# Score products of a gated attention: eight tiles of 64x32 in place of four of 64x64

## The chip, the cores and the metric

The kernel runs on one core of a Trainium2 chip. The metric is the device time of one execution in microseconds (us); the time of a kernel is the median of its runs. TensorE multiplies matrices (its weight loads are shown as an engine of their own, PEld), VectorE (DVE), ScalarE (ACT) and GpSimd (POOL) work elementwise, and SyncE (SP) issues most DMAs. Matrix products land in PSUM, in eight banks of 128 partitions x 512 float32 values.

## The reference

Gated linear attention (batch 4, 8 heads, 768 positions, 48 values a head) is followed by a two-layer block with a piecewise activation:

```python
f = 1.0 / (1.0 + np.exp(-f_logit))
for t in range(S):
    state = f[:, :, t, :, None] * state + np.einsum('bhd,bhe->bhde', k[:, :, t], v[:, :, t])
    y[:, :, t] = np.einsum('bhd,bhde->bhe', q[:, :, t], state)
x = y.transpose(0, 2, 1, 3).reshape(B * S, H * D)          # 3072 x 384
h = x @ w_in                                               # 3072 x 2048
g = np.where(h >= 1, h, np.where(h <= -1, 0.0, (h + 1) ** 2 / 4))
return g @ w_out                                           # 3072 x 384
```

All of it is wanted to float32 accuracy.

## The kernel before, in words

The 768 positions are cut into six steps of 128 (`C`), for all four batches, so that a step has 512 columns (`N`). For each step the attention yields 512 rows of x, and the two-layer block follows as 16 units, one for each 128 of the 2048 hidden values: 96 units in all. A unit's first half (`unit_1`, line 265) multiplies x by a slice of `w_in`; ScalarE and VectorE apply the activation; its second half (`unit_2`, line 289) adds its product with a slice of `w_out` to three PSUM banks. x, the weights and the activations are split into a high and a low part of a reduced float32, so that each half has nine matmuls of 512 columns.

The recurrence is not run position by position. Keys and queries of a step are scaled by running products of the gate. Within blocks of 64 positions (`T`) the outputs come from masked products of keys with queries, across blocks from the state. The heads stand in pairs on the partitions, head 0 at 0 to 47 and head 1 at 64 to 111, and pairs are taken two at a time. For each two pairs of steps 1 to 5, that is ten times, these steps run on TensorE:

- `scores_of_two` (line 657), which the change touches: products of 64 keys with 64 queries, float32, for 2 pairs x 4 batches x 2 heads x 2 blocks of keys. A matmul loads the keys (48 rows for the head's values x 64 columns) and streams 64 queries. Block 0 of the keys goes to PSUM partitions 0 to 63 and block 1 to 64 to 127; head 0 goes to a bank lent by the units (`ph`) and head 1 to one of three banks of the attention's own (`pa`). Head and block fix the place in the array, so that the four matmuls of a batch lie on four different tiles of 64 rows and 64 columns. VectorE then multiplies by the mask (line 663).
- `begin` (line 712): masked products times values, for the part that crosses over, and `states_by_parts` (line 791), the state's new part, at a later visit.
- `outputs` (line 739, then line 712 again): queries times states, and the rest of the masked products times values.

`transpose_tensor` (line 676) turns the keys of four early pairs; later ones are turned on VectorE. Lines 579, 609, 821, 836 and 770 belong to step 0.

The order is worked out ahead by a planner (`Plan`): it has a cost for each kind of work (the table `COST`, where `both` stands for `scores_of_two`) and puts the operations of every engine in an order, TensorE's in the order in which the program adds them. Each visit of the attention stands after a given unit (`TURNS`, `VISITS`). From the fourth two pairs on, line 739, line 712 and line 657 follow one another in TensorE's order with nothing between. A float32 matmul is one row in the program's order; the profile records it as two matmuls, each with its weight load.

Of the kernel before, what the change touches and what calls it, by code (L numbers as in the profile page):

```python
# [22 lines left out]
B, H, S, D = 4, 8, 768, 48  # L23
# [7 lines left out]
HEADS = ((0, 48), (64, 112))  # L31
# [8 lines left out]
T = C // 2  # L40
# [14 lines left out]
            rows=316, turned_rows=150, scan=1140, dve=602, small=200, sums=467, gate=600, act=575, bits=660, round=485, copy=520, turned=412, sig=538, decay=226,  # L55
# [27 lines left out]
class Plan:  # L83
# [7 lines left out]
    def add(self, engine, cost, emit, *deps, kb=0, near=0):  # L91
        flat = []

        def spread(d):
            if isinstance(d, list):
                for e in d:
                    spread(e)
            elif d is not None and d not in flat:
                flat.append(d)

        spread(list(deps))
        cost, kind = COST[cost] if isinstance(cost, str) else cost, cost
        if engine == "PE":
            if self.tensor is not None and self.tensor not in flat:
                flat.append(self.tensor)
            small = kind in SMALL_PRODUCTS
            cost += (COST["last"] if small else COST["first"]) if small != self.small else 0
            self.small = small
        o = Op(engine, cost, emit, flat, kb, near)
        for d in flat:  # L110
            d.users.append(o)
        if engine == "PE":
            self.tensor = o
        self.ops.append(o)
        return o
# [66 lines left out]
def gla_moe(ctx: ExitStack, tc: tile.TileContext, ff, kqd, f0, vv, vad, vbd, wd, fixedd, gates, values, headsd, out):  # L182
    nc = tc.nc
# [38 lines left out]
    half, up, down, top_of = (const.tile([128, 1], F32, name=a) for a in ("half", "up", "down", "top_of"))  # L222
# [4 lines left out]
    def wide(a):  # L227
        return a.rearrange("r b c -> r (b c)")

    def part(t, k):  # L230

        return t[:, k * N:(k + 1) * N].rearrange("r (b c) -> r b c", b=B)
# [8 lines left out]
    def key(n, p, b):  # L241
        return part(kq[p], 0)[:, B - 1 - b]

    def query(n, p, b):
        return part(kq[p], 1)[:, b]
# [63 lines left out]
    def vec(cost, fn, *deps):  # L309
        return add("DVE", cost, fn, *deps)  # L310
# [141 lines left out]
    def old(n, *names, of=att):  # L452

        return [] if n < 0 else [of[n].get(k) for k in names]
# [104 lines left out]
    def blocks(n):  # L559

        return [(pairs[n][1], m) for m in range(B)]
# [66 lines left out]
    def by_block(t):  # L628

        return wide(t).rearrange("u (o t) -> u o t", t=T)  # L630

    def masked(n):

        return [by_block(t) for t in am[n // 2 % 2 * 2:][:2]]

    TILES = ((0, 0), (1, 1), (1, 0), (0, 1))

    def borrowed(k):

        return [(6, ph[(k + 1) % 2].rearrange("p (b c) -> p b c", b=B), [gs[k - 1]["3"]]), bank(2)]  # L640

    def freed(k, held, *by):

        lent[k + 1] = by[0]
        banks[held[1][0]] = [by[1]]

    def scores_of_two(n, k):

        c, d = att[n], att[n + 1]
        held = borrowed(k)  # L650

        def emit():
            for e in range(2):
                for m, (q, b) in enumerate(blocks(n + e)):
                    for k, h in TILES:
                        (a, z), half = HEADS[h], slice(T * k, T * k + T)
                        nc.tensor.matmul(by_block(held[h][1])[half, e * B + m], key(n + e, q, b)[a:z, half],  # L657
                                         query(n + e, q, b)[a:z, T * (1 - k):][:, :T], start=True, stop=True)

        c["sc"] = d["sc"] = add("PE", "both", emit, c["kq"], d["kq"], [h[2] for h in held])  # L660
        c["am"] = d["am"] = []
        for h, (b, ps, _) in enumerate(held):
            o = vec("dve", lambda h=h, ps=ps: nc.vector.tensor_tensor(
                out=masked(n)[h], in0=by_block(ps), in1=mask_t.rearrange("u (o t) -> u o t", o=1).broadcast_to([C, 2 * B, T]), op=ALU.mult),
                c["sc"], ready["mask_t"], old(n - 4, "y"), att[2]["y"], att[2]["st"])
            c["am"].append(o)
        freed(k, held, *c["am"])
# [372 lines left out]
    with tc.If(bad > 0):  # L1040
# [7 lines left out]
        with tc.For_i(0, S, 1) as t:  # L1048
            e, z, y = tmp
            vb, fkq, z = e[:R, 0:768], e[:R, 768:816], z[:R, 0:768]  # L1050
# [22 lines left out]
        with tc.For_i(0, NI, 1) as i:  # L1073
# [9 lines left out]
            for j in range(NJ):  # L1083
                s, a, hi, lo = (t[j % 2] for t in (ph, act, ghi, glo))
# [89 lines left out]
```

## Time and profile before

| what | value |
|---|---|
| median of three runs (lowest, highest) | 472.98 us (472.7, 473.71) |
| the profiled execution: its own time | 474.75 us |
| its span, first to last instruction | 472.9 us |
| mean granted TensorE clock | 0.996 |
| TensorE busy, matmul records | 463.3 us, 4551 |
| VectorE busy | 369.0 us |
| ScalarE busy | 265.2 us |
| the ten calls of line 657, one call | 1.11 to 1.16 us |

The span is what the profile shows between the first and the last instruction; the execution's own time has a little more around it. "PE" is TensorE's matmuls and "PEld" its weight loads. In the grouped view a row reads: line, engine, operation, output<-inputs, shapes, count, then busy us and the mean ns of one, then the idle time of the engine just before, and what ended it. A shape such as `48*64 48x64` is the loaded operand (48 rows, 64 columns), and then what is streamed. In the timeline a row begins with the start and the duration in us. In the view by stretches a row holds the stretch, its length, the busy time of the engines with their counts, the granted clock, and the DMA's share and GB/s.

### The profile page before, as it was taken

The page shows a single profiled execution, that of the slowest core. Times are in us where ns is not written, and L with a number is a line of the kernel's source. Part 1 is how long each engine was busy: PE and PEld are TensorE (multiplying, and loading weights), DVE is VectorE, ACT ScalarE, POOL GpSimd, SP SyncE. Part 2 cuts the span into 40 slices and gives each one's busy share as a digit, 9 for nine tenths or more (in the row PEclk, how much of TensorE's full clock was granted, in tenths as well). Part 3 has the DMA queues.
Part 4 walks back from the last instruction along what each step waited for, and adds up shares of the span by engine and source line. Part 5 has one row for each costly group of instructions (what it writes and reads, how often), then busy time and mean ns, then how long its engine had stood idle before and what let it go on. Part 6 is the DMA issues. An engine that isn't in the chain of part 4 may idle for free.

```text
span 472.9 us, 10962 instructions
## 1 busy us (share of the span) xinstructions
PE 463.3 (98%) x4551; PEld 378.2 (80%) x4551; DVE 369.0 (78%) x704; ACT 265.2 (56%) x483; POOL 25.1 (5%) x67
## 2 busy tenths in 40 slices
PE   8999999999999999999999999999999999999993
PEld 4787888888888888888888888888888888888883
DVE  6989998999999988999889879566675645655553
ACT  3589989964463654645545464645464445544451
POOL 4100010010000001002000002000000000000000
PEclk9999999999999999999999999999999999999998
DMA  8788858372030332401234050333113342422322
GB/s 295 241 265 277 271 159 282 119 195 77 11 115 34 104 77 80 147 2 46 60 86 136 1 171 22 104 70 107 68 47 90 91 93 82 150 86 90 89 89 74
DMA packets 21336, 54.39 MB, mean 115 GB/s; under 512 B 3328, under 2 KB 5504, under 8 KB 21280
## 3 DMA queue, kind: packets, MB, share of 16 engines
q1 hardware_dynamic: 21184, 53.53, 36.6%
q8 instruction: 37, 0.61, 0.5%
q14 instruction: 19, 0.16, 0.1%
q10 hardware_dynamic: 96, 0.10, 0.1%
HBM read 44.76 MB, written 4.72 MB: 105 GB/s over the span
## 4 chain that ended last, share of the span: by engine, by line
PE 91%; DMA 3%; DVE 2%; ACT 1%; issue 1%; SPq 0%; DVEq 0%; ACTq 0%
PE po L289 41%; PE ph L265 40%; DMA raw<-in_w 2%; PE pa L712 2%; PE pa L739 2%; PE ph L657 2%; DMA f<-in_f 1%; PE pa L791 1%; PE ph L791 1%; DVE w L487 1%; PE pa L657 0%; ACT bits L395 0%; PE pa L836 0%; DVE am L622 0%; PE pa L821 0%
## 5 line engine op out<-in xcount | busy, mean ns | idle before, releaser
L265 PE MATMUL ph<-x,w_hi 128*128 128x512 f32 x570 | 145.3, 390 | 0.2 <-ACT w_hi L401 0.2
L268 ACT ACTIVATE act<-ph,half 128x512 f32<-128x512 f32 x96 | 66.0, 687 | 118.0 <-PE ph L265 115.2
L265 PEld LDWEIGHTS ph<-x,w_hi 128*128 128x128 f32 x570 | 106.8, 188 | 23.1 <-ACT w_hi L401 0.6
L276 DVE SCALAR_TENSOR_TENSOR act<-ph,act 128x512 f32<-128x512 f32 x96 | 66.1, 688 | 60.0 <-ACT act L271 58.6
L279 ACT CAST ghi<-act 128x512 fp32r<-128x512 f32 x96 | 59.6, 621 | 57.9 <-DVE act L276 57.8
L289 PE MATMUL po<-ghi,w_hi 128*128 128x512 f32 x287 | 85.6, 400 | 0.4 <-ACT ghi L279 0.4
L289 PE MATMUL po<-ghi,w_lo 128*128 128x512 f32 x287 | 82.8, 390 | 0.0
L289 PE MATMUL po<-glo,w_hi 128*128 128x512 f32 x287 | 82.5, 389 | 0.0
L265 PE MATMUL ph<-x,w_lo 128*128 128x512 f32 x285 | 80.0, 389 | 0.0
L282 DVE TENSOR_TENSOR glo<-act,ghi 128x512 fp32r<-128x512 f32 x96 | 66.1, 688 | 15.8 <-ACT ghi L279 13.6
L690 DVE STREAM_TRANSPOSE kn<-kq 32x128 f32<-32x128 f32 x224 | 67.8, 303 | 3.6
L289 PEld LDWEIGHTS po<-ghi,w_lo 128*128 128x128 f32 x287 | 53.9, 188 | 11.5
L289 PEld LDWEIGHTS po<-glo,w_hi 128*128 128x128 f32 x287 | 53.9, 188 | 11.5
L265 PEld LDWEIGHTS ph<-x,w_lo 128*128 128x128 f32 x285 | 53.5, 188 | 11.1
L271 ACT ACTIVATE act<-act 128x512 f32<-128x512 f32 x96 | 60.7, 632 | 2.8
L289 PEld LDWEIGHTS po<-ghi,w_hi 128*128 128x128 f32 x287 | 52.1, 188 | 11.6 <-ACT ghi L279 0.6
L414 DVE TENSOR_REDUCE ok<-raw 128x1 f32<-128x512 f32 x48 | 31.4, 679 | 1.8 <-DMA raw<-in_w 1.5
L487 DVE TENSOR_TENSOR_SCAN w<-f,least_w 128x512 f32<-128x512 f32 (+1 forms) x18 | 20.7, 1157 | 2.1 <-ACT f L483 2.1
L491 POOL COPY end<-w 128x4 f32<-128x4 f32 (+1 forms) x20 | 8.4, 419 | 259.3 <-DVE w L487 259.1
L494 DVE TENSOR_TENSOR_SCAN f<-f,rec 128x512 f32<-128x512 f32 (+1 forms) x18 | 20.7, 1156 | 0.1
L395 ACT ACTIVATE bits<-raw,top_of 128x512 uint32<-128x512 fp8e4 (+1 forms) x25 | 18.5, 743 | 3.9 <-DMA raw<-in_w 3.9
L555 ACT ACTIVATE sd<-sd,kq 112x48 f32<-112x48 f32 x80 | 19.4, 325 | 0.0
(120 smaller groups left out, 381.6 us busy)
## 6 DMA issues: line engine op xcount, KB each, us to landing
raw<-in_w SPq DMA_DIRECT2D x21, 511.6 KB, 4.5
kq<-in_kq SPq DMA_DIRECT2D x18, 512.0 KB, 5.4
raw<-in_w SPq DMA_DIRECT2D x18, 512.0 KB, 3.6
out_y<-raw SPq DMA_DIRECT2D x17, 256.0 KB, 2.2
f<-in_f SPq DMA_DIRECT2D x16, 256.5 KB, 3.3
v<-in_v SPq DMA_DIRECT2D x10, 384.0 KB, 5.3
raw<-in_w SPq DMA_DIRECT2D x12, 256.0 KB, 3.0
kq<-kq SPq DMA_DIRECT2D x30, 64.2 KB, 2.7
```

The source lines that it names most:

```text
L265: nc.tensor.matmul(ps[:, to], w_in(w_hi if high else w_lo, j, kt), xt[:, kt, t, c], start=(n == 0), stop=(n == 8))
L268: nc.scalar.activation(a, ps, AF.Relu, bias=half, scale=0.5)
L271: nc.scalar.activation(a, a, AF.Square)
L276: nc.vector.scalar_tensor_tensor(out=a, in0=ps, scalar=1.0, in1=a, op0=ALU.max, op1=ALU.min)
L279: nc.scalar.copy(hi, a)
L282: nc.vector.tensor_tensor(out=lo, in0=a, in1=hi.bitcast(F32), op=ALU.subtract)
L289: nc.tensor.matmul(po[e][:, c], w_out(part, j, e), g[:, of], start=(j == 0 and n == 0 and c.start == 0), stop=(j == NJ - 1 and n == 2))
L414: seen.append(vec("dve", lambda z=z, op=op: nc.vector.tensor_reduce(out=ok[:, 1 + NG + z + c:2 + NG + z + c], in_=words_of(raw[2])[1].bitc ...
L487: s1 = vec(COST["scan"] if count == 1 else 602, lambda bwd=bwd, u0=u0, u1=u1: nc.vector.tensor_tensor_scan(out=wide(w[:, u0:u1]), data0=bw ...
L494: s2 = vec(COST["scan"] if count == 1 else 602, lambda fwd=fwd, b0=b0, b1=b1: nc.vector.tensor_tensor_scan(out=fwd, data0=fwd, data1=wide( ...
L555: nc.scalar.activation(ds[:, at + b * D:at + (b + 1) * D], state[:, p * B + b], AF.Copy, scale=whole(kq[p])[:R, b:b + 1])
L690: nc.vector.transpose(kn[n % 2][u:u + 32, ::-1, r:r + 32], src[:, :, u:u + 32])
```

## The change

Each matmul of `scores_of_two` with 64 keys becomes two of 32. `u` counts the four blocks of 32 keys, and `c` makes the head alternate, so that the eight matmuls of a batch go to eight tiles of 64 rows and 32 columns, in the order (0, 0), (3, 1), (1, 1), (2, 0), (0, 1), (3, 0), (1, 0), (2, 1) of block and head. The queries are the same 64 as before, `1 - u // 2` in place of `1 - k`. What is computed, where it lands in PSUM, and the masking are the same. A call has 64 matmuls in place of 32.

```diff
-                    for k, h in TILES:
-                        (a, z), half = HEADS[h], slice(T * k, T * k + T)
-                        nc.tensor.matmul(by_block(held[h][1])[half, e * B + m], key(n + e, q, b)[a:z, half],
-                                         query(n + e, q, b)[a:z, T * (1 - k):][:, :T], start=True, stop=True)
+                    for u, h in [(u, (u + c) % 2) for c in range(2) for u in (0, 3, 1, 2)]:
+                        (a, z), rows = HEADS[h], slice(32 * u, 32 * u + 32)
+                        nc.tensor.matmul(by_block(held[h][1])[rows, e * B + m], key(n + e, q, b)[a:z, rows],
+                                         query(n + e, q, b)[a:z, T * (1 - u // 2):][:, :T], start=True, stop=True)
```

The planner's costs are as they were, so the order of all other work is too: the rows of VectorE, ScalarE, GpSimd and SyncE are the same in both programs, and TensorE has 2723 rows where it had 2563. At the fourth call, where line 657 follows line 712 (`ph` and `pa` are PSUM banks, `kq` holds keys and queries, `am` masked products, `v` values), TensorE's order was:

```order
L712 MATMUL pa_107<-am_76,v 48x64
L712 MATMUL pa_108<-am_77,v 48x64
L657 MATMUL ph_110<-kq_70 64x64
L657 MATMUL pa_109<-kq_70 64x64
L657 MATMUL ph_110<-kq_70 64x64
L657 MATMUL pa_109<-kq_70 64x64
L657 MATMUL ph_110<-kq_70 64x64
```

and is now:

```order
L712 MATMUL pa_107<-am_76,v 48x64
L712 MATMUL pa_108<-am_77,v 48x64
L657 MATMUL ph_110<-kq_70 32x64
L657 MATMUL pa_109<-kq_70 32x64 x2
L657 MATMUL ph_110<-kq_70 32x64
L657 MATMUL pa_109<-kq_70 32x64
L657 MATMUL ph_110<-kq_70 32x64 x2
L657 MATMUL pa_109<-kq_70 32x64
```

The sizes are partitions x columns of the output. What stood as four rows of 64x64 for a batch is eight matmuls of 32x64 (x2 is two in a row on the same bank), and no instruction of another line has moved between them. At the end of the same call stood, of the second pair (`kq_71`), with the unit that follows:

```order
L657 MATMUL ph_110<-kq_71 64x64
L657 MATMUL pa_109<-kq_71 64x64
L289 MATMUL po_112<-ghi_88,w_hi 128x512
L289 MATMUL po_113<-ghi_88,w_hi 128x512
L289 MATMUL po_114<-ghi_88,w_hi 128x512
```

and stands now:

```order
L657 MATMUL pa_109<-kq_71 32x64
L657 MATMUL ph_110<-kq_71 32x64 x2
L657 MATMUL pa_109<-kq_71 32x64
L289 MATMUL po_112<-ghi_88,w_hi 128x512
L289 MATMUL po_113<-ghi_88,w_hi 128x512
L289 MATMUL po_114<-ghi_88,w_hi 128x512
```

The same unit follows, behind 64 matmuls of the call in place of 32.

## The prediction

> **What bounds the kernel now.** I read the page's engine totals and its chain first, to learn which engine a change has to move.
>
> ```profile
> span 472.9 us, 10962 instructions
> PE 463.3 (98%) x4551; PEld 378.2 (80%) x4551; DVE 369.0 (78%) x704; ACT 265.2 (56%) x483; POOL 25.1 (5%) x67
> q8 instruction: 37, 0.61, 0.5%
> PE 91%; DMA 3%; DVE 2%; ACT 1%; issue 1%; SPq 0%; DVEq 0%; ACTq 0%
> ```
>
> TensorE is busy for 98% of the span and makes 91% of the chain, so whatever its stream gains or loses in the changed step is gained or lost at the end; nothing else covers it. Two other numbers matter below: each of the 4551 matmul records has one weight load, so TensorE executes 9102 instructions, and 37 instruction fetches brought 0.61 MB, one fetch of 16.5 KB for some 250 instructions.
>
> The changed step is line 657. The grouped view and the view by stretches give its size.
>
> ```profile
> L657 PE MATMUL ph<-kq 48*64 48x64 f32 x320 | 11.3, 219 | 0.0
> L657 PEld LDWEIGHTS ph<-kq 48*64 48x64 f32 x320 | 10.3, 135 | 0.6 <-issue 0.4
> L836 PEld LDWEIGHTS po<-kn,v 128*32 128x32 f32 x8 | 0.8, 109 | 0.0
> ...
> 0.00:60.00 60.00, 1.16 (x64) 1.02 (x64) 1.00 0.82 270
> 140.00:165.00 25.00, 1.11 (x64) 1.03 (x64) 1.00 0.28 88
> ```
>
> The step runs ten times. Each call of 32 matmuls shows 64 records (a float32 matmul is recorded as two passes, each with its load) and takes 1.11 to 1.16 us. All ten are 11.3 us, 2.4% of the span: that is all there is to win, and nothing bounds a loss. Inside a call the timeline shows what sets the pace:
>
> ```profile
> 54.53 0.22 PE L657 MATMUL ph<-kq 48*64 48x64 f32 x1
> 54.53 0.22 PE L657 MATMUL pa<-kq 48*64 48x64 f32 x1
> 54.54 0.22 PE L657 MATMUL ph<-kq 48*64 48x64 f32 x1
> 54.55 0.22 PE L657 MATMUL pa<-kq 48*64 48x64 f32 x1
> 54.58 0.22 PE L657 MATMUL ph<-kq 48*64 48x64 f32 x1
> ...
> 54.99 0.22 PE L657 MATMUL ph<-kq 48*64 48x64 f32 x1
> ```
>
> Four records start within 20 ns, one on each tile (about 7 ns apart), and then all four tiles wait: the next four begin at 54.58. From 54.53 to 54.99 there are 8 rounds, 58 ns each. Two neighbouring steps with other shapes tell what a round consists of:
>
> ```profile
> 60.23 0.03 PE pa L791
> ...
> 60.86 0.03 PE pa L791
> ...
> 136.36 1.04 PE pa L739 x64
> 137.40 0.45 PE pa L712 x32
> ```
>
> Line 791 (48 columns loaded, 48 streamed) needs 45 ns a round (14 rounds from 60.23 to 60.86), line 712 (48 loaded, 64 streamed) 56 ns (0.45 us for 8 rounds). So the streamed columns set a round, and loading 64 columns instead of 48 adds about 2 ns.
>
> **The change part by part.** *The rounds.* 64 matmuls make 128 records and 128 loads in a call, twice as many, on eight tiles. Each tile still runs 16 records of 64 streamed columns: 16 rounds remain. With 32 columns to load, the streaming alone sets the round, as at line 712: 56 instead of 58 ns, over 15 rounds -0.04 us a call. Eight starts at 7 ns fill 53 ns of a 56 ns round, so they just fit; the last round's starts end 27 ns later than with four, +0.03 us. Halving the work of a tile's load buys nothing more, since the load already lies beside the streaming. Over ten calls: -0.15 us. If a round stayed at four starts, a call would need 32 rounds and 0.93 us more; that is the upper bound (a rival below).
>
> [...]
>
> *The change of tile size.* Seven of the ten calls follow line 712 directly, whose 48 columns stand on 64-column tiles; there the array now goes from 64- to 32-column tiles. Before, the loader never idled there (line 657 shows 0.4 us of "issue", once). The nearest rows:
>
> ```profile
> 19.38 0.14 PEld L836 LDWEIGHTS po<-act,v 128*32 128x32 f32 x2 [0.17 <-issue]
> ...
> L739 PEld LDWEIGHTS pa<-kq,y 48*48 48x48 f32 x320 | 5.2, 119 | 3.5 <-issue 3.5
> ```
>
> At 19.38 us the array goes from 64 to 32 columns and the loader idles 0.17 us; at line 739, coming from the full array, 0.35 us each of ten times, of which a 512-column matmul covers most. Bounds 0 and 0.35; I take 0.12, near the first row less the 0.04 between matmuls anyway: 7 x 0.12 = +0.8 us. The other three calls, and the exits, change tile size already.
>
> *The instruction stream.* This is the part that decides. The change adds 640 matmul records and 640 loads, 1280 instructions. Most of the program needs one instruction in 113 ns (9 matmuls and 9 loads in 2.04 us), but the bursts of lines 739, 712 and 657, seven of them, use 320 in 2.4 us and will use 448 in the same time. Instructions come in fetches of some 250, and the trace has one place where they did not come in time, just after the last burst:
>
> ```profile
> 354.86 0.30 PEld L265 LDWEIGHTS ph<-x,w_hi 128*128 128x128 f32 x2 [0.45 <-issue]
> ...
> GB/s 149 149 1043 298 0 0 0 0 1 0 0 0 0 0 0 0 0 0 0 0 0 0 0 0 0 0 0 0 0 0 0 0 0 0 0 0 0 0 0 0
> q8 instruction: 1, 0.02, 5.5%
> ...
> GB/s 0 0 0 596 0 0 0 0 0 0 0 0 0 0 0 0 0 0 0 0 0 0 0 0 0 0 0 0 0 0 0 0 0 0 0 0 0 0 0 149
> q8 instruction: 1, 0.02, 5.4%
> ```
>
> These two DMA windows are 352.3 to 353.4 and 355.9 to 357 us, 40 slices each. The first fetch starts in the third slice, 352.37; TensorE, in the middle of a unit of six matmuls with no wait in it, idles 0.45 us until 354.86; the next fetch follows at 356.0. I read this as two blocks of instructions: a fetch starts when the sequencer enters the second, and the sequencer stops if it reaches its end too soon. Starved, one block takes 3.6 us from fetch to fetch (1 us moving, 1.5 until the first instruction, 1.15 until the next fetch).
>
> The sequencer runs ahead of the array, and that lead is the cover:
>
> ```profile
> L657 PEldq EVENT_SEMAPHORE x1: 51/51/51, 101.6 to 101.6; - x1
> 101.83 0.64 PEld L289 LDWEIGHTS po<-glo,w_hi 128*128 128x128 f32 x3
> 102.51 1.32 PEld L265 LDWEIGHTS ph<-x,w_hi 128*128 128x128 f32 x6
> 103.87 0.64 PEld L265 LDWEIGHTS ph<-x,w_lo 128*128 128x128 f32 x3
> 104.87 0.13 PEld L657 LDWEIGHTS ph<-kq 48*64 48x64 f32 x1 [0.35 <-issue]
> ```
>
> It handled line 657's wait at 101.6 us, over 12 matmuls and their loads before the step, so it leads by some 30 instructions: 3.4 us in the long matmuls, 0.1 us inside a burst. A block that ends inside a burst therefore stalls TensorE. Where blocks end follows from the counts (matmuls before each of the seven bursts, and before the idle place):
>
> ```profile
> 0.00:136.28 136.28, 133.95 (x1410) 1.00 0.60 192
> 0.00:160.91 160.91, 158.58 (x1756) 1.00 0.55 175
> 0.00:193.67 193.67, 191.34 (x2138) 1.00 0.51 160
> 0.00:230.50 230.50, 228.17 (x2538) 1.00 0.45 143
> 0.00:275.49 275.49, 273.16 (x2974) 1.00 0.43 134
> 0.00:300.08 300.08, 297.75 (x3320) 1.00 0.41 129
> 0.00:349.16 349.16, 346.83 (x3742) 1.00 0.39 123
> 0.00:354.84 354.84, 352.51 (x3915) 1.00 0.39 122
> ```
>
> A block ends at instruction 2 x 3915 = 7830, the others at multiples of 256 from there (I take 256 as the round number nearest to 250). Each call ahead adds 128. So the bursts now begin at 3204, 4024, 4916, 5844, 6844, 7664 and 8636, and blocks end 18 and 274 instructions into the first, 222 and 478 into the second, then 98 and 354, 194 and 450, 218 and 474, 166 and 422, 218 and 474. The sequencer's own waits are in the stream but not in the counts; they move these places up by at most 20. Less the lead of 30, three bursts (the 1st, 3rd, 6th) hold a whole block, and the 4th ends one at its very end. The others finish their second block after the burst, behind 3.4 us of long matmuls that cover the wait.
>
> The price is 3.6 us less the time in which the burst uses the block: 7 ns an instruction in lines 739 and 712, 3.5 in line 657, less 0.1 of lead. First: 1.5 us to use, stall 2.0. Third: 1.3, stall 2.2. Sixth: 1.1, stall 2.4. Fourth: 1.0, less 1.3 of cover, stall 1.3. Together 7.9 us. A fetch can also meet data traffic: the one of 352.37 was due at 349.6 (the block before 7830 ends 60 instructions of 7 ns behind the 7484 of 349.16, less the lead), 2.8 us instead of 1.15, so 0 to 1.65 us more each; I take 0.3 for each of four, +1.2.
>
> **The sum.** -0.15 + 0.8 + 7.9 + 1.2 = +9.7 us. The profiled execution took 474.75 us with 1.85 outside its span, and becomes 484.5; the median of the runs is 472.98, 1.8 below it, and becomes **482.7 us**. Own range: without the fourth stall, and each other 0.4 shorter, 478.5; with the full delay of every fetch, 488.
>
> **The rivals.** *Fetches keep up* (chance 0.12): more than two blocks are held, and the idle 0.45 us at 354.86 had another cause. Then -0.15 + 0.8: 473.6 us, no measurable change. For it: one starved place in the whole trace. Against it: that place waited for nothing else, and the next fetch came after it and not before. [...]
>
> *Shorter loads win* (0.06), on the other side: the tile change drains for nothing, since the loader starts while other tiles still stream, and fetches keep up. From there the 0.04 us a call decides, at most 0.45 with no late last round: 472.5 us. Against it: the loader's idle 0.17 us at 19.38.
>
> *Eight tiles run no faster than four* (0.10): the starts of a round do not all fit, or loads and streams of four column tiles in the same 64 rows hinder each other. 640 more records at 58/4 = 14.6 ns: +9.3 us. Blocks are then used more slowly in line 657, stalls fall to some 1.6 x 3 + 0.6: 472.98 + 9.3 + 0.8 + 5.4 + 1.2 = 490 us. Against it: 7 ns starts; for it, the trace never shows more than four.
>
> **Chances.** The forecast has 0.68, and 0.04 stays for slight losses between (474 to 478). A measurement of this kernel tells 0.2% (0.95 us) from no change: slower 0.83, same 0.14, faster 0.03. The range that leaves out 2 in 10 goes from 473.5, half of the first rival, to 490.
>
> **What would show it.** Right: line 657 with 640 records for each bank at 32 columns, starts 7 ns apart in groups of eight, rounds of 56 ns; 42 fetches; idle "issue" of some 2 us inside line 657 in the bursts near 138, 197 and 305 us, with one behind a burst near 236, and none in the three single calls before 110 us. Wrong: calls of 1.1 us everywhere without such idle time (blocks are deeper), calls of 2 us everywhere (tiles or starts), or idle time in other bursts (my places are off).

## The result, and the profile after

| | before | changed |
|---|---|---|
| median (lowest to highest), us | 473.42 (472.7 to 474.16), 6 runs | 485.69 (484.18 to 487.71), 6 runs |
| ratio, 95% interval | | 1.0257 (1.0241 to 1.0273) |
| the profiled execution, us | 474.75 | 485.13 |
| its span, us | 472.9 | 483.4 |
| mean granted TensorE clock | 0.996 | 0.991 |

The change makes the kernel 12.3 us slower; 482.7 was forecast, +9.7. The profiled pair differs by 10.4 us. One run below counts as slow, one of the four with half the queries (489.27 us), and its ratio leaves that run out. Of the page of the changed kernel, the totals, the fetches and the chain; and of its grouped view, the changed line (the columns as before):

```profile
span 483.4 us, 12242 instructions
PE 470.7 (97%) x5191; PEld 383.3 (79%) x5191; DVE 368.9 (76%) x704; ACT 265.1 (55%) x483; POOL 24.9 (5%) x67
q8 instruction: 42, 0.69, 0.6%
PE 94%; ACT 2%; DMA 1%; issue 1%; DVE 1%; ACTq 0%
...
L657 PE MATMUL pa<-kq 48*32 48x64 f32 x640 | 15.8, 226 | 3.3 <-issue 3.3
L657 PE MATMUL ph<-kq 48*32 48x64 f32 x640 | 15.8, 226 | 0.0
```

640 matmuls and 640 loads more, and 5 fetches more, as the edit says. TensorE still is the chain. What is new is 3.3 us of idle time inside line 657, ended by nothing that the profile shows.

**The idle places.** Behind 45 us, TensorE's loader waits 0.35 us at each of some twenty changes of tile size, in both kernels. Apart from these it has four waits of more than 0.2 us, at the rows that begin with these loads (idle time in the brackets):

```profile
199.58 0.10 PEld L657 LDWEIGHTS ph<-kq 48*32 48x32 f32 x1 [1.83 <-issue]
...
239.48 0.19 PEld L289 LDWEIGHTS po<-ghi,w_lo 128*128 128x128 f32 x1 [0.91 <-issue]
...
287.58 0.19 PEld L265 LDWEIGHTS ph<-x,w_lo 128*128 128x128 f32 x1 [0.27 <-issue]
...
310.79 0.12 PEld L657 LDWEIGHTS pa<-kq 48*32 48x32 f32 x1 [1.77 <-issue]
```

Two are inside the calls of the third and the sixth burst, one lies behind the fourth, as forecast; the first burst has none, and one behind the fifth was not forecast. How many matmuls had started by then is in the view by stretches:

```profile
0.00:199.00 199.00, 196.59 (x2639) 1.00 0.49 158
0.00:239.20 239.20, 236.00 (x3151) 1.00 0.43 141
0.00:287.30 287.30, 283.82 (x3661) 1.00 0.42 134
0.00:310.00 310.00, 305.64 (x4045) 1.00 0.39 126
```

In instructions (the loads counted one by one, 5279, 6302, 7323 and 8090, and 7830 at the idle place of the kernel before) these are 150 to 159 modulo 256. The trace also has the sequencer's own waits, 33, 34, 37 and 38 up to these places and 42 up to the old one. With them all five are 192 modulo 256 exactly. The fetches count the same: 5 more for 1280 instructions more is one for 256. So I take 256 for the size of a block, with TensorE run dry at the end of one each time.

**The calls.** The same view for line 657 alone; in the second and third stretch stand calls of the fifth and the third burst (1.11 us each before, 1.16 in the first stretch):

```profile
0.00:60.00 60.00, 1.48 (x128) 1.32 (x128) 1.00 0.80 273
280.00:290.00 10.00, 1.49 (x128) 1.32 (x128) 1.00 0.54 184
195.00:205.00 10.00, 1.75 (x128) 1.44 (x128) 1.00 0.40 147
```

A call is 0.32 us longer where it stands alone and 0.38 in a burst (fifth burst), although nothing is idle there; the third burst's 1.75 us hold one of the idle places, at which the call runs dry and fills again. Its timeline shows why (start, duration; x2 is two in a row):

```profile
360.67 0.24 PE L657 MATMUL ph<-kq 48*32 48x64 f32 x1
360.67 0.25 PE L657 MATMUL pa<-kq 48*32 48x64 f32 x2
360.69 0.24 PE L657 MATMUL ph<-kq 48*32 48x64 f32 x1
360.69 0.24 PE L657 MATMUL pa<-kq 48*32 48x64 f32 x1
360.70 0.25 PE L657 MATMUL ph<-kq 48*32 48x64 f32 x2
360.71 0.24 PE L657 MATMUL pa<-kq 48*32 48x64 f32 x1
360.75 0.22 PE L657 MATMUL ph<-kq 48*32 48x64 f32 x1
```

Eight start within 50 ns, the next eight begin at 360.75, and the two rounds from there take 57 and 55 ns: eight tiles do run together, in the 56 ns of a round at line 712. That lasts for some 32 matmuls and their loads. From then on the eight starts of a round take some 67 ns or more (from the trace, the rounds of this call: 79, 57, 55, 76, 148, 66, 67, 78, 102, 67, 66, 68, 94, 85, 67 ns).

**The way in.** Line 712 starts 0.45 us before line 657 in the kernel before (276.43 to 276.88) and 0.56 us now:

```profile
281.84 0.63 PE L712 MATMUL pa<-am,v 64*48 64x64 f32 x32
282.40 0.24 PE L657 MATMUL ph<-kq 48*32 48x64 f32 x1
```

**The clock.** In the view by stretches, the third column behind the length is the clock that TensorE was granted:

```profile
305.00:309.00 4.00, 4.00 (x219) 1.00 0.15 20
311.10:314.20 3.10, 3.10 (x18) 0.51 0.73 177
314.20:320.00 5.80, 5.80 (x27) 1.00 0.39 69
```

At the idle place of 310.8 the clock is halved for 3.4 us (310.72 to 314.13 in the trace); seven long matmuls fall into it, most of which start 0.427 us apart instead of 0.226.

**The sum of the profiled pair.** Three lone calls 3 x 0.32 = 1.0; seven in bursts 7 x (0.38 + 0.11) = 3.4; lesser delays in three of them, 0.4 (the first burst's call shows 1.76 us, two others 1.54 and 1.56); idle places 4.8 less the 0.45 of before, 4.3; half clock 7 x 0.2 = 1.4. Together some 10.5 us, and the span grew by 10.5. That they meet so closely is luck: the profiled run of the changed kernel reached its first call 0.7 us earlier (53.45 against 54.13 us), so that 0.6 us of what comes after has no term here.

### The profile page after: what moved, and what is told of

It is laid out like the page before. It is cut to its first block, busy times and chain, and to the rows that moved or that the text cites. A ratio compares the mean times of both kernels' runs of the same rounds, so it can differ in the third digit from the quotient of the medians.

```text
span 483.4 us, 12242 instructions
## 1 busy us (share of the span) xinstructions
PE 470.7 (97%) x5191; PEld 383.3 (79%) x5191; DVE 368.9 (76%) x704; ACT 265.1 (55%) x483; POOL 24.9 (5%) x67
## 4 chain that ended last, share of the span: by engine, by line
PE 94%; ACT 2%; DMA 1%; issue 1%; DVE 1%; ACTq 0%
PE po L289 41%; PE ph L265 39%; PE pa L712 2%; PE ph L342 2%; PE pa L739 2%; PE ph L657 2%; PE pa L657 1%; DMA raw<-in_w 1%; PE pa L791 1%; PE ph L791 1%; PE ph L609 1%; PE ph L864 0%; ACT bits L395 0%; PE po L579 0%; PE pa L836 0%
## 5 line engine op out<-in xcount | busy, mean ns | idle before, releaser
L289 PEld LDWEIGHTS po<-glo,w_hi 128*128 128x128 f32 x287 | 54.1, 189 | 11.5
L265 PEld LDWEIGHTS ph<-x,w_lo 128*128 128x128 f32 x285 | 53.5, 188 | 11.3 <-issue 0.3
```

The costliest lines, as they stand in the source:

```text
L265: nc.tensor.matmul(ps[:, to], w_in(w_hi if high else w_lo, j, kt), xt[:, kt, t, c], start=(n == 0), stop=(n == 8))
L289: nc.tensor.matmul(po[e][:, c], w_out(part, j, e), g[:, of], start=(j == 0 and n == 0 and c.start == 0), stop=(j == NJ - 1 and n == 2))
```

## The experiments

Two theories stood against each other. **F**: instructions come too slowly, at the end of a block (fetch) and within a call (dispatch). **T**: the tiles are slow, eight of 32 columns hinder each other. Where a median of the kernel before is needed, it is that of the same chip: 473.77 us for the first four runs, 473.71 for the next two.

### The same program, 64 instructions later

```diff
+    def first():
+        warm(12)
+        for _ in range(32):
+            nc.tensor.matmul(ph[1][:, 0:1], zeros, zeros[:, 0:1], start=True, stop=True)
-    add("PE", 4000, lambda: warm(12), set_zeros)
+    add("PE", 4000, first, set_zeros)
```

> The changed kernel with 32 one-column matmuls of zeros (64 instructions) more in the warm-up, before the first product, where TensorE waits for data. Theory F (instructions do not come in time: blocks of 256, and a stall where a block begins and ends inside a burst): every block now ends 64 instructions earlier in the program, so a whole block lies in the second, fourth, fifth, sixth and seventh burst and no longer in the third. Five stalls of 1.9 us (9.5 us) in place of the present 4.6 us: 490.6 us against 485.7, and the idle places still stand at an instruction count of 192 modulo 256, the sequencer's waits counted. Theory T (the loss is in the tiles: eight tiles of 32 columns hinder each other): nothing changes, 485.7 us, and the idle places stay in the same calls.

Measured: 496.13 us, ratio 1.0491 (1.0455 to 1.0526). The idle rows of its loader (the changed line is 662 here), and the matmuls started by then:

```profile
167.99 0.10 PEld L662 LDWEIGHTS ph<-kq 48*32 48x32 f32 x1 [1.26 <-issue]
...
202.10 0.10 PEld L662 LDWEIGHTS ph<-kq 48*32 48x32 f32 x1 [1.43 <-issue]
...
242.90 0.10 PEld L662 LDWEIGHTS pa<-kq 48*32 48x32 f32 x1 [1.33 <-issue]
...
290.04 0.10 PEld L662 LDWEIGHTS ph<-kq 48*32 48x32 f32 x1 [1.52 <-issue]
...
316.37 0.10 PEld L662 LDWEIGHTS pa<-kq 48*32 48x32 f32 x1 [1.50 <-issue]
...
368.77 0.10 PEld L662 LDWEIGHTS ph<-kq 48*32 48x32 f32 x1 [2.48 <-issue]
```

```profile
0.00:202.00 202.00, 196.64 (x2640) 1.00 0.48 155
0.00:242.80 242.80, 236.27 (x3151) 0.99 0.43 138
0.00:289.90 289.90, 282.03 (x3661) 0.99 0.41 129
0.00:316.30 316.30, 307.03 (x4045) 0.99 0.39 124
```

The places moved in the program and did not move in the count: 3151, 3661 and 4045 matmuls again, though what stands there is 64 instructions earlier in the program. All six are at 192 modulo 256 with the waits. The second, fourth, fifth, sixth and seventh burst stall as expected; the third, which I expected to be spared, stalls too (its block begins 43 instructions into the burst, just behind my lead of 30). Idle time is 9.5 us in place of 4.8. Of the 6.9 us by which the profiled execution (492.0) exceeds that of the changed kernel, 4.7 are these, where I expected 4.9. Another 2.1 lie ahead of the first call, which begins at 55.6 us instead of 53.5. The added matmuls are hardly the reason: they start between 5.8 and 6.5 us, and TensorE is only 0.3 us behind the changed kernel at 26 us. It then waits for ScalarE, which had itself waited 3.1 us for a weight transfer:

```profile
40.68 0.50 PE L289 MATMUL po<-ghi,w_hi 128*128 128x512 f32 x1 [1.89 <-ACT ghi L279]
```

That is not the effect that was asked for: without an edit there, the first call of the other runs began anywhere from 52.5 to 54.1 us. The median lies 10.4 us above that of the changed kernel and 5.5 above F. The profiled run was the fastest of the four: 492.0, 494.49, 497.76 and 499.36 us went with mean clocks of 0.993, 0.987, 0.983 and 0.980, so part of what the profiled run does not show is half clock; how much, no trace here tells. T has no answer to the idle places.

### Half the queries, three quarters of them

```diff
-                        nc.tensor.matmul(by_block(held[h][1])[rows, e * B + m], key(n + e, q, b)[a:z, rows],
-                                         query(n + e, q, b)[a:z, T * (1 - u // 2):][:, :T], start=True, stop=True)
+                        nc.tensor.matmul(by_block(held[h][1])[rows, e * B + m, 0:32], key(n + e, q, b)[a:z, rows],
+                                         query(n + e, q, b)[a:z, T * (1 - u // 2):][:, :32], start=True, stop=True)
```

> The changed kernel with 32 queries streamed in place of 64 in line 657; the other half of each product is left out. Theory F with a dispatch of some 5 ns an instruction: as many instructions, so a call still lasts 1.25 us from first to last start, and the stalls stay: 485.2 us. Theory T (streams of eight tiles hinder each other, a call is bound by what it streams): a call falls from 1.27 to some 0.9 us, 7 ns a start, and the kernel by 10 x 0.37 us to 482 us or less.

Measured: 485.75 us (481.59 to 489.27), ratio 1.0208 (1.0167 to 1.0248): halving what the tiles stream wins nothing that can be told from the times. The calls by themselves, and the starts in one of them:

```profile
280.00:290.00 10.00, 1.29 (x128) 1.18 (x128) 1.00 0.59 197
...
285.05 0.23 PE L657 MATMUL ph<-kq 48*32 48x32 f32 x3
285.08 0.21 PE L657 MATMUL pa<-kq 48*32 48x32 f32 x2
...
285.31 0.23 PE L657 MATMUL ph<-kq 48*32 48x32 f32 x3
```

From 285.05 to 285.31 stand 32 matmuls, 8.3 ns each; the trace has ten rounds of 66 or 67 ns in a row, 16 instructions of 4.17 ns. The same loads and matmuls need less while they are queued (the second and third round of this call take 40 and 32 ns), so I read this as the pace at which instructions are handed out. A call fell by 0.17 us to 1.10 from first to last start, where F said 1.25 and T 0.9: read so, dispatch is the floor, and what is streamed adds to it. The ten calls gave back 1.7 us, and the idle places took it: 1.70, 2.80, 2.10 and 0.51 us, 7.1 in place of 4.8. The longest:

```profile
241.65 0.19 PEld L289 LDWEIGHTS po<-ghi,w_lo 128*128 128x128 f32 x1 [2.80 <-issue]
```

What the streaming adds was asked again with 48 queries (the same edit with 48 in place of 32):

> The changed kernel with 48 queries streamed in place of 64 (the last 16 columns of each product are left out). If the 0.17 us by which a call with 64 queries is longer than one with 32 comes from streaming that nearly fills a round (56 of 67 ns), 48 queries (45 ns) leave room and a call takes 1.10 us. If it grows with what is streamed: 1.18 us.

1.17 us from first to last start (the first rounds 67, 47 and 42 ns, the last ten 67 with an 85, a 71 and an 81 between): the extra grows with what is streamed, 0.17 us at 64 columns, 0.08 at 48. Of the 0.17 us, 0.07 stand in the first three rounds (191 ns against 125; the second and third take 57 and 55 against 40 and 32); nothing in the fourth and fifth together (224 against 223); and 0.09 in the last ten, most of it in two neighbouring rounds of each four. Why there, no run tells. 484.8 us in one run.

### Twice the matmuls on four tiles

```diff
-                    for k, h in TILES:
+                    for k, h in TILES + TILES:
```

> The kernel before with every matmul of line 657 issued twice on its tile of 64x64: as many instructions as the change has, without eight tiles or 32 columns. Theory F: a call takes 32 rounds of 58 ns, +0.93 us, +9.3 us in all; the blocks end at the same instructions as in the changed kernel, so that TensorE stalls in the third and sixth burst for some 1.5 us each (the calls are longer and hide more), 473.4 + 9.3 + 3 = 486 us, with idle places at 192 modulo 256 again. Theory T: only the rounds are longer, 482.7 us, and no idle time inside a call.

Measured: 488.02 us, ratio 1.0297 (1.0279 to 1.0315), 2 us above F. Its idle places:

```profile
202.22 0.13 PEld L657 LDWEIGHTS pa<-kq 48*64 48x64 f32 x1 [1.66 <-issue]
...
242.34 0.19 PEld L289 LDWEIGHTS po<-ghi,w_lo 128*128 128x128 f32 x1 [0.52 <-issue]
...
291.02 0.19 PEld L265 LDWEIGHTS ph<-x,w_lo 128*128 128x128 f32 x1 [0.35 <-issue]
...
314.47 0.13 PEld L657 LDWEIGHTS ph<-kq 48*64 48x64 f32 x1 [1.62 <-issue]
```

These are the four places of the changed kernel, at the same instructions (5279, 6302, 7323, 8090), without eight tiles, without 32 columns and without a change of tile size. More instructions in the burst are enough. 4.2 us of idle time where I expected 3 makes somewhat over half of the difference.

### Half the matmuls on narrow tiles

```diff
-                    for u, h in [(u, (u + c) % 2) for c in range(2) for u in (0, 3, 1, 2)]:
+                    for u, h in [(u, u % 2) for u in (0, 3, 1, 2)]:
```

> The changed kernel with four of the eight matmuls of a batch (one head for each block of 32 keys; the other four are left out): as many instructions as before, on tiles of 32 columns. Theory F: only the change of tile size is left, seven times 0.16 us (the first start comes 0.11 us later, and the first round is not hidden, 0.05): 474.5 us, calls of 0.95 us from first to last start. Theory T: tiles of 32 columns are slow themselves, so that half of the loss stays: 479 us.

Measured: 474.38 us, ratio 1.0014 (1.0001 to 1.0027). Line 712 starts 0.55 us before line 657 (0.45 before), a call shows

```profile
340.00:360.00 20.00, 1.10 (x64) 0.94 (x64) 1.00 0.18 55
```

and no long idle place is left, the old one of 0.45 us included. So narrow tiles and the way into them cost some 0.6 us net (0.05 to 1.3 by the interval); nearly all of the loss is in the number of instructions. Only four of the eight tiles are used here; that eight run together is shown by the rounds of 56 ns, not by this run.

### The calls moved away from the bursts

```diff
-VISITS = {..., 10: (23, 25, 28), 12: (28, 32, 35), 14: (35, 41, 43), 16: (43, 47, 53), 18: (53, 56, 58), 20: (58, 64, 69), 22: (69, 73, 74)}
+VISITS = {..., 10: (24, 25, 28), 12: (29, 32, 35), 14: (36, 41, 43), 16: (44, 47, 53), 18: (54, 56, 58), 20: (59, 64, 69), 22: (70, 73, 74)}
```

> The changed kernel with line 657 of the last seven calls one unit later than lines 739 and 712, so that 18 long matmuls and their loads stand between them; as many instructions, the same eight tiles. Theory F: no block lies wholly in a burst any more (192 instructions, then 256 behind 3.4 us of long matmuls): the idle places of 1.9, 1.8, 0.6 and 0.2 us and the half clock behind one of them go, and the calls keep their 1.27 us, which is dispatch at 4.2 ns an instruction. Against the same move made to the kernel before (next run): +10 x 0.32 = +3.2 us, 478 us. Theory T (the tiles, or the calls by themselves, cause the idle time): it moves along with the calls, 486 us.

> The kernel before with the same move, as a control: seven more changes of tile size on the way in (0.10 us each, as a call behind line 265 shows) and out (0.11), less the 0.3 us of the one idle place: 473.5 + 1.5 - 0.3 = 474.7 us by either theory.

Measured: 480.85 us for the changed kernel, ratio 1.0151 (1.0131 to 1.0171), 476.99 for the kernel before, ratio 1.0063 (1.0046 to 1.008). Both are 2 to 3 us above what I expected. Some 1.1 us of it is an omission: the second way out of a burst also costs 0.11 us at the unit's first matmul (in the trace 0.337 us until the second one starts, 0.226 between others), and the first round of the call is no longer hidden, 0.05, seven times each. The rest I did not trace. The difference of the two is 3.9 us, of the profiled pair 3.4, where F said 3.2. In the grouped view of the changed kernel with its calls apart:

```profile
L657 PEld LDWEIGHTS ph<-kq 48*32 48x32 f32 x640 | 13.5, 105 | 3.1 <-issue 2.5 <-DVE kn L690 0.4
```

The 2.5 us are seven changes of tile size of 0.35 us; no long wait is left in the timeline, and the clock stays whole. The three calls that stood alone before take 1.48 us as in the changed kernel. Of the seven that were moved, one does, and six take 1.51 to 1.74; here the longest and that of 1.48:

```profile
165.00:171.00 6.00, 1.74 (x128) 1.51 (x128) 1.00 0.63 144
283.00:289.00 6.00, 1.48 (x128) 1.32 (x128) 1.00 0.77 269
```

Together the six have 0.7 us more, short delays inside the calls that F did not have; with the 3.2 they come to 3.9. With as many instructions on the same tiles, the change costs 3.9 us here and 12.3 in the bursts.

### Another order of the eight

```diff
-                    for u, h in [(u, (u + c) % 2) for c in range(2) for u in (0, 3, 1, 2)]:
+                    for u, h in [(u, c) for c in range(2) for u in range(4)]:
```

> The changed kernel with another order of the eight matmuls of a batch: the four blocks of keys of head 0, then those of head 1. What is asked is the length of a call that stands alone (1.27 us from first to last start in the changed kernel, 1.10 with half the queries, 0.94 before). If dispatch alone sets it: 1.27 us again. If matmuls that follow one another on the same 64 rows hinder each other: longer, 1.4 us or more.

1.27 us from first to last start again, round by round within 2 ns of the changed kernel. This order of the tiles changes nothing. The single run took 487.51 us; its trace has two stretches of half clock, behind each of the two long idle places:

```profile
200.40:203.80 3.40, 3.40 (x9) 0.51 0.76 244
313.40:316.50 3.10, 3.10 (x8) 0.50 0.64 159
```

## Why the prediction was right, and where it was off

*The bound.* Right: TensorE carried the chain before and after, and what its stream lost, the span lost.

*The instruction stream.* My reading, blocks of 256 and a stall where a whole block falls inside a burst, is borne out in the main: by long idle places at 192 modulo 256 in every run that has them, by their staying at the count when the program is shifted, by their coming back on four tiles, and by their going when the calls are moved away. That two blocks are held was an estimate from one idle place; it fits every place, and no run asked it by itself.

The size was off. I took 7.9 us for four stalls (2.0, 2.2, 2.4, 1.3) and 1.2 for data traffic; the profile has 1.8, 1.8, 0.9 and 0.3. The first stall did not come, and its fetch was early: the DMA view of the changed kernel has the packet in slice 21 of 40 between 135.5 and 136.35 us, before the burst began (136.6 us).

```profile
GB/s 0 0 0 0 0 0 0 0 0 0 0 0 0 0 0 0 0 0 0 0 771 0 0 0 0 0 0 0 0 0 0 0 0 0 0 0 0 0 0 0
q8 instruction: 1, 0.02, 7.2%
```

This block begins 37 instructions into the burst, at 136.85 us; if its fetch starts when the sequencer comes to the block, as I read it, the lead is more than my 30 instructions at times. The burst did not go free: its call shows 1.76 us instead of 1.49. The others were smaller since calls use up a block at 5 ns an instruction, not 3.5, which hides more.

*The rounds.* This is the step that failed: "Eight starts at 7 ns fill 53 ns of a 56 ns round, so they just fit", -0.15 us over ten calls. The eight do start 7 ns apart and rounds of 56 ns do occur, but only for the first 32 matmuls or so of a call. I took the spacing of four ready matmuls for a pace that could be kept up. Kept up, a matmul and its load take 8.3 ns at best (with half the queries), and with 64 columns 9.9 on average (1.27 us for 128): +3.2 us instead of -0.15. (The two parts of that term, -0.04 and +0.03 a call, make -0.1 over ten calls; and what the lower end of my own range leaves out, 1.3, 1.2 and all of the 1.2 for data traffic, gives 479.0 and not 478.5. Nothing hangs on either.) Part of what I charged to fetches belongs here. So the total came close in part by luck: fetches cost 4.3 us where I had 9.1, and the calls, the half clock and the lesser delays, for which I had next to nothing, brought 5.0.

*The change of tile size.* Forecast 0.8; 0.11 us at each of seven calls and 0.05 for a first round that is no longer hidden, 1.1, of which the run with half the matmuls shows 0.6 net.

*Not foreseen.* The half clock: 1.4 us in the profiled execution. It makes the changed kernel's times spread (484.18 to 487.71): runs with a mean clock of 0.996 and 0.988 took 484.18 and 486.4 us, but one with 0.990 took 487.71, so the clock is not all of it. What else differs from run to run stays open. Of the 1.9 us between the 10.4 of the profiled pair and the 12.3 of the medians, 1.3 are on the side of the kernel before, whose profiled execution (474.75) took longer than any of its six timed runs.

*The rivals.* "Fetches keep up" and "shorter loads win" fall with the idle places. "Eight tiles run no faster than four" falls with the rounds of 56 ns; its extra 9.3 us would have shown as calls of 2 us.

No run here beats the kernel before, and the 8.3 ns a matmul that a call kept up at best says why: at that pace 128 of them take 1.07 us, while the 64 of four tiles take 0.94. What helped the changed kernel, calls apart from the bursts, costs the kernel before 3.3 us.

## What to carry to other kernels

Cutting these small float32 matmuls over twice as many tiles left a round's streaming as it was (56 ns for eight tiles, 58 for four) and doubled the instructions; here 1280 more instructions cost 2.6%, where narrow tiles and the way into them cost some 0.6 us. Before such a step, count what the engine must be handed, not only what it must compute: the starts at the head of a call (here eight in 56 ns) show the pace of what is already queued, and those further on (eight in 66 ns at best) the pace that is kept up. Where many short instructions stand together, count them against the block in which they are fetched (here 256), and put long instructions between the groups: the same change cost 3.9 us where long matmuls stood between, and 12.3 in the bursts.

## What the runs showed of the hardware

- Further into a call that did not stall, matmuls and loads together started one in 4.17 ns at best (66.7 ns for 16, with 32 streamed columns and in the shortest later rounds with 48 and 64). At the head of a call they started closer, with their loads between: 8 matmuls in 56 ns with 64 streamed columns, 8 in 32 ns with 32. That the first is the pace of dispatch, and the second that of what is already queued, is my reading.
- TensorE's instructions came in fetches of 16 KB, 37 before and 42 with 1280 instructions more: 256 each. At the five idle places at the end of a block in the two kernels, one before and four after, TensorE went on 2.3 to 2.6 us after an instruction fetch had started, and that fetch had started 0.8 to 2.8 us after the array began the block before; what sets that delay, no run tells. A block used up in 1.5 to 1.6 us left the engine idle for 1.8 us in the changed kernel, twice; one used up in 1.7 us (the first burst) left it idle for none, and there the fetch had started 0.9 us before the array came to the block. The longest wait was 2.80 us, with half the queries.
- The clock of the changed kernel fell to half once inside the run, for 3.41 us (310.72 to 314.13 us), 303.79 us after the full clock had first come, which is 89 times that length. At the end of the kernel before, it fell 464.21 us after, 136 times that length. The 3.41 us just before 310.72 held 1.54 us without a matmul and no long matmul (512 columns). The 3.41 us that hold most of the other long idle place, 198.08 to 201.49, counted off in the same way, held 1.50 us without a matmul and 1.30 us of long ones, and no half clock followed; what made the difference, no run asked. Of the two idle places inside line 657, both were followed by half clock with 48 queries (0.50 and 0.51 granted) and with the other order (0.51 and 0.50), one in the changed kernel (0.51) and with half the queries (0.50); of the six in the shifted program, one (0.50).
- A round on one tile took, by streamed and loaded columns: 64 and 48, 56 ns (line 712); 64 and 64, 58 (line 657 before); 48 and 48, 45 (line 791); 48 and 32, 42 (line 657 with 48 queries, at the head of a call); 32 and 32, 32 (with half the queries, likewise). Eight tiles kept the 56 ns side by side for the first rounds of a call.
